# A gated recurrence feeding four expert layers: the first unit's work spread over four engines, the second group's input split earlier, and later units' scores set next to the unit ahead

## The chip, the cores and the metric

One core of one Trainium2 chip. The metric is the device time of one execution in microseconds (us), lower is better. "Start-to-start" is the time from the start of one matmul to the start of the next on TensorE, taken from the trace; a pace is its mean over a stream, without waits and half-speed stretches.

## The reference

Four batches, eight heads, 768 time steps, head width 48. A recurrence with a per-channel decay gives 3072 rows of 384; four experts with 1024 hidden columns are applied to every row and merged with normalised weights.

```python
for t in range(S):
    state = alpha[:, :, t, :, None] * state + einsum('bhd,bhe->bhde', k[:, :, t], v[:, :, t])
    y[:, :, t] = einsum('bhd,bhde->bhe', q[:, :, t], state)
x = y.transpose(0, 2, 1, 3).reshape(B * S, H * D)
p = domain_probs / (domain_probs.sum(-1, keepdims=True) + 1e-09)
for e in range(E):
    h = np.maximum(x @ w1[e], 0.0)
    out += p[:, e:e + 1] * (h @ w2[e])
```

## The kernel before

The rows are cut into 24 **units** of 128 rows (six time blocks of four batches), and the units into groups. A group's units first go through the recurrence (`attention(u)`, 17 steps that the scheduler hands out one by one), which leaves x, then through the experts. While the experts of group g run, the recurrence of group g + 1 is fed in between: `deal` gives every step of every unit a time, and `advance` emits it when the estimated clock has reached it. A step's instructions stand in each engine's program where `advance` emits them, and that place is all that a "time" means.

From the second group on, x, w1, w2 and the hidden layer are each split into three parts (w2 and the hidden layer of the second group only in part), and every product of split operands is three faster matmuls instead of a slow one (for down 3 x 175 ns, where the unsplit product shows as two records 323 ns apart). In what follows **up** is the product with w1 (512 columns of x stream, w1 is stationary) and **down** is the product with w2 (384 columns of w2 stream, the hidden layer is stationary).

The parts that the change touches:

```python
BEATS = [*(0.055 * (j + 1) for j in range(11)), 0.69, 0.75, 0.8, 0.87, 0.94, 1.0]

def attention(u):                                  # each yield ends a step
    nc.scalar.copy(out=AT, in_=turned(pair(ra)))   # turned: 4 transposes on TensorE
    ...
    nc.scalar.copy(out=KT, in_=turned(pair(rk)))
    nc.vector.tensor_mul(own, rq[:, :, :D], rk[:, :, :D])
    nc.vector.reduce_sum(out=dot, in_=own, axis=AX.X)
    yield
    nc.vector.tensor_mul(QT, turned(pair(rq)), AT)
    yield
    # seven levels: copy_q (ScalarE), next_q, next_k
    def next_q(li):
        nc.vector.tensor_mul(qv, qv, spread(dv[:, :, :, 0], m))
        dec = work.tile([P, NP, P // (2 * m)], F32, name=f"dec{li}", bufs=1)
        nc.vector.tensor_mul(dec, dv[:, :, :, 0], dv[:, :, :, 1])
    def next_k(li):
        nc.scalar.copy(out=new[:, :, :, 1, :], in_=old[:, :, :, 1, :])
        nc.vector.tensor_mul(new[:, :, :, 0, :], ...)
    ...   # scores (sc) of levels 0-3, later far (level 6) and sc of levels 4-5
    for s in range(2):                             # lat <- near
        nc.scalar.copy(out=lat[rows, :, rows], in_=near[rows])
    ...   # result (yps), keys turned back
    if cb < NCB - 1:                               # state product and update
        sps = ps.tile([P, NP, 2, D], F32, name="sps", tag="w")
        for p in range(NP):
            nc.tensor.matmul(sps[:, p], lhsT=KB[:, p, :], rhs=rv[:, 2 * p:2 * p + 2, :D], ...)
        for i in range(2):
            rows = slice(HD * i, HD * (i + 1))
            old, add = st[rows, :, i, :], sps[rows, :, i, :]
            ...
# deal(): a unit's window [begin, end] and its 17 steps in it
events += [(begin + (end - begin) * beat, u, run) for beat in BEATS]
# start: the constants and the domain probabilities on the ACT queue, the rest on SP
nc.scalar.dma_start(out=p_all, in_=moe_domain_probs.rearrange("(n p) e -> p n e", p=P))
load(0, "akqv"); load(1, "akqv")
# the last slot's down stage of a group: the next group's x is split in between
for step, at in enumerate((0.0, 0.6, 0.7, 0.78)):
    ... between.append((at, lambda step=step: split_x(after[0], step)))
```

The state product uses only the two diagonal blocks of what it computes: head pair p with values of both heads gives four blocks, and two are read.

## Time and profile before

| | before |
|---|---|
| time, median of 3 | 1064.21 us (1062.67 to 1064.66) |
| span of the profiled run | 1062.8 us |
| TensorE busy | 98% of it |
| first expert matmul | 26.22 us |
| up matmuls of 512 columns, start-to-start | 229.8 ns, 1440 of them |
| down matmuls with split operands, start-to-start | 175.0 ns, 1872 of them |

The prediction shows the table by stretches: its columns are the stretch, its length, then busy us and instructions of TensorE, of weight loads, VectorE, ScalarE and GpSimd, then granted clock, DMA share and GB/s.

```profile
150.00:175.00 25.00, 22.89 (x139) 15.36 (x138) 20.55 (x41) 13.81 (x32) 2.68 (x5) 0.93 1.01 380
```

The number to look at is 0.93: in these 25 us TensorE's granted clock was not full.

The timeline of an up stream (start, duration, engine, line, work):

```profile
517.92 1.53 PE L546 MATMUL one<-xT,w 128*128 128x512 f32 x6
...
519.98 1.53 PE L546 MATMUL one<-xT,w 128*128 128x512 f32 x6
```

Nine matmuls take 519.98 - 517.92 = 2.06 us. A stream's pace is read from starts like these. The busy time of the group hides it: it counts overlapping durations.

### The profile page before, as it was taken

The numbers are of one execution on the slowest core, as the hardware profiler recorded it, in microseconds if no ns is written. First come the engines' busy times: TensorE is split into PE (matmuls) and PEld (weight loads), VectorE is DVE, ScalarE is ACT, GpSimd is POOL, SyncE is SP. The second block draws the span as 40 slices with busy tenths as digits, with TensorE's granted clock in tenths as the row PEclk, the third lists the DMA queues.
The fourth block names the chain that finished last, engine by engine and source line by source line (L and its number), as shares of the span: only waits on it lengthen the run. The fifth ranks groups of instructions, "written<-read, shape, count | busy, mean of one in ns | idle before, by whom it ended". The sixth has DMA issues, their size and how long they took to land.

```text
span 1062.8 us, 21599 instructions
## 1 busy us (share of the span) xinstructions
PE 1041.9 (98%) x8508; PEld 906.2 (85%) x8508; DVE 781.6 (74%) x1619; ACT 569.0 (54%) x1202; POOL 32.9 (3%) x71
## 2 busy tenths in 40 slices
PE   8899999999999999999999999999999999999998
PEld 7777776687788898898898998988989889898988
DVE  5488777677779877778877877986877875666565
ACT  5687875665756555536546435555464443323232
POOL 2010010000001000000000000000000000000000
PEclk9999999999999999999999999999999999999999
DMA  8596799797977957758669559586594454444531
GB/s 124 157 325 202 245 318 352 272 339 241 307 256 271 376 180 276 279 165 315 249 187 364 201 190 339 172 307 231 167 373 174 194 208 170 187 179 178 197 160 45
DMA packets 158838, 251.66 MB, mean 237 GB/s; under 512 B 120113, under 2 KB 135345, under 8 KB 136209
## 3 DMA queue, kind: packets, MB, share of 16 engines
q1 hardware_dynamic: 149600, 208.82, 57.3%
q0 software_dynamic: 5760, 41.29, 9.7%
q8 instruction: 67, 1.10, 0.4%
q10 hardware_dynamic: 3376, 0.17, 0.3%
q14 instruction: 35, 0.28, 0.1%
HBM read 207.79 MB, written 42.47 MB: 235 GB/s over the span
## 4 chain that ended last, share of the span: by engine, by line
PE 85%; ACT 5%; DVE 5%; DMA 2%; issue 2%; SPq 1%; ACTq 0%; DVEq 0%
PE ops L639 36%; PE one L546 23%; PE two L546 11%; PE sc L338 6%; PE yps L432 3%; PE tp L270 3%; ACT qb L312 2%; PE one L538 1%; PE sps L467 1%; PE far L393 1%; DMA hT<-in_moe_w_dram 1%; DVE w L230 1%; ACT KT L330 1%; DMA rq<-in_q_dram 1%; SPq L214 1%
## 5 line engine op out<-in xcount | busy, mean ns | idle before, releaser
L639 PE MATMUL ops<-w,hT 128*128 128x384 f32 x1872 | 347.4, 340 | 0.2 <-DVE hT L592 0.2
L639 PEld LDWEIGHTS ops<-w,hT 128*128 128x128 f32 x1872 | 325.4, 188 | 4.7 <-ACT t L557 0.6
L546 PE MATMUL one<-xT,w 128*128 128x512 f32 x960 | 254.4, 400 | 2.7 <-DVE xT L252 2.3
L546 PEld LDWEIGHTS one<-xT,w 128*128 128x128 f32 x960 | 176.3, 189 | 42.2 <-DVE xT L252 4.0
L557 ACT ACTIVATE t<-one 128x512 f32<-128x512 f32 (+1 forms) x192 | 107.2, 558 | 180.7 <-PE one L546 175.3
L312 ACT COPY qb<-QT 64x256 f32<-64x256 f32 x336 | 136.6, 407 | 71.2 <-DVE QT L293 42.7
L586 DVE SCALAR_TENSOR_TENSOR hT<-t,hT 128x512 fp32r<-128x512 f32 (+1 forms) x172 | 110.5, 643 | 68.3 <-ACT hT L584 65.8
L559 DVE TENSOR_TENSOR t<-t,two 128x512 f32<-128x512 f32 (+1 forms) x172 | 109.5, 636 | 58.0 <-ACT t L557 29.3
L584 ACT ACTIVATE hT<-t 128x512 fp32r<-128x512 f32 (+1 forms) x172 | 101.8, 592 | 86.4 <-DVE t L559 85.3
L546 PE MATMUL two<-xT,w 128*128 128x512 f32 x480 | 136.9, 394 | 0.0
L546 PEld LDWEIGHTS two<-xT,w 128*128 128x128 f32 x480 | 90.6, 189 | 20.2 <-DVE acc L668 0.2
L639 PE MATMUL ops<-hT 128*128 128x384 f32 x288 | 100.9, 491 | 0.3 <-DMA hT<-in_moe_w_dram 0.3
L592 DVE SCALAR_TENSOR_TENSOR hT<-hT 128x512 fp32r<-128x512 f32 (+1 forms) x172 | 101.0, 634 | 0.0
L348 DVE COPY_PREDICATED near<-masks,sc 128x256 f32<-128x256 uint8 x144 | 76.9, 534 | 19.2 <-PE sc L338 16.3
L319 DVE TENSOR_TENSOR QT<-QT,dec 128x256 f32<-128x256 f32 x144 | 60.8, 423 | 36.0 <-ACT qb L312 35.3
L338 PEld LDWEIGHTS sc<-qb,KT 128*64 128x64 f32 x2304 | 72.7, 138 | 9.3 <-issue 4.7
L338 PE MATMUL sc<-qb,KT 128*64 128x64 f32 x2304 | 77.2, 223 | 2.6 <-ACT qb L312 2.6
L639 PEld LDWEIGHTS ops<-hT 128*128 128x128 f32 x288 | 52.1, 190 | 29.6 <-DMA hT<-in_moe_w_dram 0.9
L668 DVE SCALAR_TENSOR_TENSOR acc<-ops,p_all,acc 128x384 f32<-128x384 f32 x82 | 49.9, 615 | 30.4 <-PE ops L639 29.2
L330 ACT COPY KT<-KT 128x256 f32<-128x256 f32 x144 | 60.0, 417 | 3.1
L331 DVE TENSOR_TENSOR KT<-KT,dec 128x256 f32<-128x256 f32 x144 | 60.2, 418 | 0.0
L538 PE MATMUL one<-xT,w 128*128 128x256 f32 (+1 forms) x240 | 46.2, 340 | 0.6 <-ACT xT L448 0.6
(88 smaller groups left out, 934.2 us busy)
## 6 DMA issues: line engine op xcount, KB each, us to landing
w<-kept SPq DMA_DIRECT2D x144, 1152.0 KB
kept<-w POOLq DMA_DIRECT2D x32, 1152.0 KB, 7.9
hT<-in_moe_w_dram SPq DMA_DIRECT2D x32, 384.0 KB
w<-in_moe_w_dram SPq DMA_DIRECT2D x48, 128.0 KB
ra<-in_alpha_dram SPq DMA_DIRECT2D x23, 192.0 KB
rk<-in_k_dram SPq DMA_DIRECT2D x23, 192.0 KB
rq<-in_q_dram SPq DMA_DIRECT2D x23, 192.0 KB
out_dram<-acc POOLq DMA_DIRECT2D x18, 192.0 KB, 7.9
```

Source lines behind the costliest of these rows:

```text
L312: nc.scalar.copy(out=qb[rows, :, i, :].rearrange("p a (b r) -> p a b r", r=m), in_=qv[rows])
L319: nc.vector.tensor_mul(qv, qv, spread(dv[:, :, :, 0], m))
L330: nc.scalar.copy(out=new[:, :, :, 1, :], in_=old[:, :, :, 1, :])
L338: nc.tensor.matmul(out[HALF * s:HALF * (s + 1), 2 * p:2 * p + 2, :], lhsT=KTs[li][:, p, HALF * s:HALF * (s + 1)], rhs=qbs[li][:, p, :, QUA ...
L348: nc.vector.copy_predicated(near.rearrange("p a (b two r) -> p a b two r", two=2, r=m)[:, :, :, 1, :], mk.unsqueeze(1).broadcast_to([P, H, ...
L546: nc.tensor.matmul(out, lhsT=w[:, part, kc], rhs=x_part(gi, part, kc), start=(part == terms[0] and kc == 0), stop=(part == terms[-1] and k ...
L557: nc.scalar.activation(out=t, in_=one, func=ACT.Copy, scale=FINE)
L559: nc.vector.tensor_add(t, t, two)
L584: nc.scalar.activation(out=top, in_=x, func=ACT.Relu, scale=TRIM)
L586: nc.vector.scalar_tensor_tensor(out=low, in0=x, scalar=0.0, in1=top.bitcast(F32), op0=ALU.max, op1=ALU.subtract)
L592: nc.vector.scalar_tensor_tensor(out=dif, in0=top.bitcast(F32), scalar=1 / 4096.0, in1=low.bitcast(F32), op0=ALU.mult, op1=ALU.subtract)
L639: nc.tensor.matmul(sums[at], lhsT=h, rhs=w, start=(n == begins[at]), stop=(n == ends[at]))
```

## The change

It has four parts. **Start:** the first unit's work is spread over four engines (key copies to GpSimd, one copy to VectorE, two VectorE operations behind QT), and the load of the probabilities moves behind the units' loads on the SP queue. **Second group's x:** the splits start at 0.3 instead of 0.6 of the last down stage. **Later units:** new step times put a unit's scores beside the result and the state update of the unit ahead, and the state product is cut into half-width tiles that compute only the blocks that are read. **Offset:** four more buffers of a small tile shift x in SBUF.

```diff
+    IN_PAIRS = [*(0.0425 * (j + 1) for j in range(8)), 0.385, 0.43, 0.475, 0.52, 0.6, 0.67, 0.755, 0.84, 1.02]
+    TOGETHER = ((15, 7), (16, 11))
+    pairs_from = half + 2 * B + 1
...
+        alone = u == 0
+        if not alone:
+            own_terms()
         yield
         nc.vector.tensor_mul(QT, turned(pair(rq)), AT)
+        if alone:
+            own_terms()
...
-            dec = work.tile([P, NP, P // (2 * m)], F32, name=f"dec{li}", bufs=1)
+            dec = work.tile([P, NP, P // (2 * m)], F32, name=f"dec{li}", bufs=1 + 4 * (li == 6))
...
-                nc.scalar.copy(out=new[:, :, :, 1, :], in_=old[:, :, :, 1, :])
+                copy = nc.gpsimd.tensor_copy if alone else nc.scalar.copy
+                copy(out=new[:, :, :, 1, :], in_=old[:, :, :, 1, :])
...
-            nc.scalar.copy(out=lat[rows, :, rows], in_=near[rows])
+            copy = nc.vector.tensor_copy if alone and s else nc.scalar.copy
+            copy(out=lat[rows, :, rows], in_=near[rows])
...
+            apart_ = u + 1 >= pairs_from
+            sps = ps.tile([P, NP, 1 if apart_ else 2, D], F32, name="sps", tag="w")
             for p in range(NP):
-                nc.tensor.matmul(sps[:, p], lhsT=KB[:, p, :], rhs=rv[:, 2 * p:2 * p + 2, :D],
-                                 start=True, stop=True)
+                for i in range(2) if apart_ else [slice(0, 2)]:
+                    rows = slice(HD * i, HD * (i + 1)) if apart_ else slice(0, P)
+                    nc.tensor.matmul(
+                        sps[rows, p], lhsT=KB[:, p, rows],
+                        rhs=rv[:, 2 * p + i, :D] if apart_ else rv[:, 2 * p:2 * p + 2, :D],
+                        start=True, stop=True)
...
-            first = wanted[gi - 1] if gi > 1 else 0.0
+            first = wanted[gi - 1] - MARGIN * (2 < gi < LAST - 1) if gi > 1 else 0.0
...   # deal(): a unit's steps 7 and 11 are set to the times of steps 15 and 16 of the unit ahead
...
-        nc.scalar.dma_start(out=p_all, in_=moe_domain_probs.rearrange("(n p) e -> p n e", p=P))
...
         load(1, "akqv")
+        nc.sync.dma_start(out=p_all, in_=moe_domain_probs.rearrange("(n p) e -> p n e", p=P))
...   # five fewer rounds of filling matmuls at the start
-                    for step, at in enumerate((0.0, 0.6, 0.7, 0.78)):
+                    for step, at in enumerate((0.0, 0.3, 0.42, 0.54) if gi == 0 else
+                                              (0.0, 0.6, 0.7, 0.78)):
```

More of the change, by code (lines that the diff above doesn't have):

```diff
@@ L286, in attention, with own_terms @@
         nc.scalar.copy(out=KT, in_=turned(pair(rk)))
-        own = work.tile([P, NT], F32, name="t")[:, :H * D].rearrange("p (h d) -> p h d", d=D)
         dot = work.tile([P, H], F32, name="dot")
-        nc.vector.tensor_mul(own, rq[:, :, :D], rk[:, :, :D])
-        nc.vector.reduce_sum(out=dot, in_=own, axis=AX.X)
-        load(after, "k")
+        def own_terms():
+            own = work.tile([P, NT], F32, name="t")[:, :H * D].rearrange("p (h d) -> p h d", d=D)
+            nc.vector.tensor_mul(own, rq[:, :, :D], rk[:, :, :D])
+            nc.vector.reduce_sum(out=dot, in_=own, axis=AX.X)
+            load(after, "k")
+        alone = u == 0
+        if not alone:
+            own_terms()
         yield
         nc.vector.tensor_mul(QT, turned(pair(rq)), AT)
+        if alone:
+            own_terms()
         load(after, "q")
@@ L464, in attention @@
             KB = AT
-            sps = ps.tile([P, NP, 2, D], F32, name="sps", tag="w")
+            apart_ = u + 1 >= pairs_from
+            sps = ps.tile([P, NP, 1 if apart_ else 2, D], F32, name="sps", tag="w")
             for p in range(NP):
-                nc.tensor.matmul(sps[:, p], lhsT=KB[:, p, :], rhs=rv[:, 2 * p:2 * p + 2, :D],
-                                 start=True, stop=True)
+                for i in range(2) if apart_ else [slice(0, 2)]:
[4 more added lines that the diff above has]
+                        start=True, stop=True)
             for i in range(2):
                 rows = slice(HD * i, HD * (i + 1))
-                old, add = st[rows, :, i, :], sps[rows, :, i, :]
+                old, add = st[rows, :, i, :], sps[rows, :, 0 if apart_ else i, :]
                 if cb == 0:
@@ L692, in deal @@
         events = []
+        times = []
         t = 0.0
@@ L713, in deal @@
                 run = attention(u)
-                events += [(begin + (end - begin) * beat, u, run) for beat in BEATS]
+                pairs = u >= pairs_from
+                beats = [0.0, *(IN_PAIRS if pairs else BEATS)]
+                due_at = {-1: begin, **{j: begin + (end - begin) * beats[j + 1] for j in (7, 11, 16)}}
+                for ahead, j in TOGETHER if pairs else ():
+                    if (u > pairs_from or j == 11) and abs(times[-1][ahead] - due_at[j]) < space / 6:
+                        due_at[j] = times[-1][ahead]
+                marks = sorted(due_at)
+                times.append([])
+                for lo, hi in zip(marks, marks[1:]):
+                    times[-1] += [due_at[hi] if j == hi else
+                                  due_at[lo] + (due_at[hi] - due_at[lo]) * (beats[j + 1] - beats[lo + 1])
+                                  / (beats[hi + 1] - beats[lo + 1]) for j in range(lo + 1, hi + 1)]
+                for j, ahead in ((6, 13), (12, 15)):
+                    if times[:-1]:
+                        times[-1][j] = max(times[-1][j], times[-2][ahead] + 0.5)
+                events += [(time, u, run) for time in times[-1]]
         return sorted(events, key=lambda x: x[:2])
@@ L751 @@
         runs = [attention(u) for u in range(len(groups[0]))]
-        fill(8)
-        for u, n in ((0, 3), (0, 6), (0, 4), (0, 5), (0, 5), (0, 4), (0, 3), (1, 0), (0, 0), (0, 2),
+        fill(7)
+        for u, n in ((0, 2), (0, 3), (0, 4), (0, 5), (0, 5), (0, 4), (0, 3), (1, 0), (0, 0), (0, 2),
                      (0, 2), (1, 2), (0, 2), (1, 0), (0, 0), (0, 4), (0, 4), (0, 0)):
```

## The prediction

> **What bounds the kernel now.** I read the page first (busy shares, chain of waits), then the table by stretches, then the timeline of the two places that the diff names, and last the groups by line.
>
> From the page of the kernel before (engine, busy us, share, instructions; then the chain by engine):
> ```profile
> PE 1041.9 (98%) x8508; PEld 906.2 (85%) x8508; DVE 781.6 (74%) x1619; ACT 569.0 (54%) x1202; POOL 32.9 (3%) x71
> ...
> PE 85%; ACT 5%; DVE 5%; DMA 2%; issue 2%; SPq 1%; ACTq 0%; DVEq 0%
> ```
> TensorE is the bound: 98% busy, and 85% of the chain that ended last. So only two kinds of change can pay: TensorE must do less, or its few holes must close. The table by stretches says where those holes are:
> ```profile
> 180.00:1062.80 882.80, 877.91 (x6860) 775.18 (x6859) 654.83 (x1330) 443.25 (x921) 17.16 (x32) 1.00 0.65 236
> ```
> After 180 us TensorE idles 882.80 - 877.91 = 4.9 us in all. The other 16 us of its idle time (1062.8 - 1041.9 = 20.9) lie before 180 us. Busy hides waits inside a stream of matmuls, too, so I also looked at start-to-start times.
>
> The first hole is the start (start us, us, engine, line, work, [idle before <- releaser], from the timeline):
> ```profile
> 8.61 0.56 DVE L289 TENSOR_TENSOR t<-rq,rk 128x384 f32<-128x384 f32 x1 [8.61 <-DMA rq<-in_q_dram]
> ...
> 9.21 0.55 DVE L290 TENSOR_REDUCE dot<-t 128x8 f32<-128x384 f32 x1
> ...
> 9.68 0.68 DVE L293 TENSOR_TENSOR QT<-tp,AT 128x512 f32<-128x512 f32 x1
> ...
> 11.34 0.45 ACT L330 COPY KT<-KT 128x256 f32<-128x256 f32 x1
> 11.35 0.43 DVE L319 TENSOR_TENSOR QT<-QT,AT 128x256 f32<-128x256 f32 x1 [0.99 <-ACT qb L312]
> ...
> 23.24 1.24 ACT L410 COPY lat<-near 64x512 f32<-64x512 f32 x2 [1.14 <-DVE near L348]
> ```
> Nothing useful happens on VectorE until q lands at 8.61; the first two operations then stand ahead of QT, which everything hangs on. The first real matmul of the expert layers starts at 26.22.
>
> The second hole is the change to the second group (timeline):
> ```profile
> 165.66 0.50 PE L546 MATMUL one<-xT,w 128*128 128x512 f32 x1 [0.17 <-DVE xT L252]
> ...
> 166.99 0.50 PE L546 MATMUL one<-xT,w 128*128 128x512 f32 x1 [0.83 <-DVE xT L252]
> ...
> 168.32 2.08 PE L546 MATMUL one<-xT,w 128*128 128x512 f32 x4 [0.83 <-DVE xT L252]
> ```
> TensorE gets one part of x, waits, gets the next. From start to start 1.33 us passes where 0.23 is normal.
>
> The third thing is the two groups that the later units' change concerns:
> ```profile
> 145.29 1.03 PE L467 MATMUL sps<-rv,AT 128*128 128x96 f32 x8
> ...
> 156.32 2.08 PE L338 MATMUL sc<-qb,KT 128*64 128x64 f32 x64
> ```
> The state product (8 records; each f32 matmul shows as two) holds TensorE for 0.81 us net: I took the time from the matmul ahead of it to the one behind it after 180 us (1039 ns, the same in 11 cases to 6 ns) less one normal 229. The 64 score records hold it for 2336 - 229 = 2107 ns alone.
>
> **What the Trainium skill says.** (1) "DMA: Bandwidth & Descriptors", section "Queues, rings and completion order": each DMA engine serves its queue rows in turn, packet by packet. The trace agrees: from 4 to 7 us the ACT queue's 16-byte packets of the domain probabilities (3,072 of its 3,376 packets) run among the SP queue's packets of k and q. SP packets drop from 962 and 894 per us (at 2 and 3 us) to 248, 470 and 577 in the next three. (2) "TensorEngine Tiling (Array Packing)", section "Key Properties": changing the tiling mode drains TensorE. The trace agrees: full to narrow adds about 90 ns to the start-to-start time (322 for 229), narrow back to full shows 152 to 203. (3) "TensorE: Matmul & The Clock Gate", section "LDWEIGHTS": a weight load costs by its columns, not its rows. The trace agrees: the state product's 96-column matmuls still start 109 to 112 ns apart, like the 128-column transposes. (4) "SBUF — State Buffer", section "SBUF: two separate sides": GpSimd and VectorE share a port pair exclusively, and a VectorE operation with two SBUF inputs loses it to a GpSimd one that reads SBUF. No run here shows it yet; GpSimd only does memsets and DMA issues in this trace.
>
> **The change part by part.**
>
> *Start.* The probabilities' load moves from the ACT queue to SP, behind both units' loads. The 3,072 packets of a, k and q then run at some 930 a us from 2.0 us on and are through at 5.3 instead of 6.95; q landed 1.65 us after its last packet, so it lands near 7.0: **-1.6 us**. The two operations ahead of QT (0.56 + 0.55) move behind it; QT must still wait for its transposes (8.65 + 0.63), so that gives 9.68 - 9.35 = 0.33, of which some 0.15 returns because they now delay the next VectorE step. One of the two 0.62 us copies of L410 goes to VectorE and runs beside the other: about -0.4. The KT copies to GpSimd give nothing: at 11.34 ACT's 0.45 us copy runs beside VectorE's 0.43 us product, which the next qb copy waits for anyway. Sum -2.2 us for the first expert matmul (26.2 to about 24). But the last quarter of w1 is issued until 23.17 and its packets run to some 28.5 us; with 1.5 us of latency it lands near 30. TensorE wanted it at 30.8 before and would want it at 28.6: a stall of over a us there, part of which replaces the 1.29 us wait for AT at 31.5. I count **-1.8 us**. The five fewer rounds of filling matmuls only take up the shorter wait.
>
> *Second group's x.* The waits at 165 to 169 us are (661 - 323) + (1328 - 229) + (1330 - 229) + (594 - 229) = 2.9 us. The splits move from 0.6 to 0.3 of the last down stage, before the slot's end. But their 6 VectorE operations (4.1 us) now stand ahead of the last split of a w1 piece (160.46), whose store and reload the matmuls need at about 178; part of the gain can turn into that wait. I count **-1.8 us**.
>
> *Later units.* Working the two schedules' arithmetic through gives the order of TensorE's groups (it reproduces the 15 result-to-scores neighbours in the trace before). Result and first scores were already neighbours for 15 of the units and become so for 17; at 4003 ns together against 1988 + 2336 - 229 apart, a pair saves only 0.09 us. What is new is that the state product of units 10 to 19 runs in half-width column tiles, in the mode of the scores, and (but for unit 17) directly ahead of the next unit's far scores. It becomes 16 records like the scores', (2107 - 220 for entry and exit) / 64 = 29.5 ns each, 0.47 us instead of 0.81. 9 x 0.34 + 0.12 for unit 17, which pays entry and exit by itself: **-3.2 us**. The number of visits to a narrow mode stays 56, because before the state product ran in full mode between full-mode matmuls and switched nothing.
>
> *Offset.* The decay tile's five buffers cost SBUF, and the count looks chosen so that x stays where it was against w1: in the program before x lies at 96 and w1 at 32 modulo 128, 64 apart, and the title says 64 after. The up matmuls should stay at 2.06 us per nine (229 ns): **0**.
>
> Sum: -1.8 - 1.8 - 3.2 - 0.1 = -6.9 us, 1064.2 to 1057.3.
>
> **The rivals.** *GpSimd costs more than it saves.* VectorE is busy 1.1 to 1.3 us of each 1.41 us level at the start, mostly with two-input operations; if each GpSimd copy locks it out, six levels could lose 0.2 to 0.3 us each, 1.5 us, and the start would gain next to nothing: 1059. Against it: the copies have slack before the scores need them. *The start's gain is not held up.* If w1 also lands earlier or the stall falls in other waits, the start gives 3 us or more, and later waits for ACT and VectorE (1 to 2 us each before 90 us) shrink with it: 1054. *The gathered steps overload ACT and VectorE.* Units now do more in less time, with TensorE in order behind them; VectorE is at 0.7 to 0.9 in most stretches. If each of 13 units makes TensorE wait 0.5 us, the later gain is gone: 1063. For it: some later waits of 0.5 to 0.9 us exist (349 and 825 us). Against it: 4.9 us of idle in 880. *The offset matters.* If x did move against w1, 1440 up matmuls at 3 ns each would be 4.3 us, in either direction.
>
> **Range and chances.** The parts are small and fairly independent: start -0.5 to -3.5, x 0 to -2.9, state product -2 to -3.5, collisions 0 to +4. That gives **1057.3 us**, with 1052 to 1062 to hold 8 times in 10. 2% is 21 us, more than all holes of TensorE; **faster by over 2%: 0.01, within 2%: 0.98, slower by over 2%: 0.01**.
>
> **What would show it.** q landing near 7.0 and the first expert matmul near 24; a wait for w1 near 28 to 30; no starts 1.33 us apart at 165, but perhaps a wait on w at fc 6 of that stage; state-product records in 128*64 form, 160 becoming 240 with 160 of them narrow at some 30 ns; the up stream still 2.06 us per nine. It would be wrong if the up stream changes pace, if TensorE shows more than 3 us of new waits after 250 us, or if the early gain is swallowed by a DMA wait at 142 to 154 us, where the chain hangs on w2 for 12 us.

## The result, and the profile after

The changed kernel took 1058.97 us (median of 4, 1058.81 to 1060.18) against 1063.84 (4 runs, 1062.67 to 1064.66). The ratio is 0.9958, 95% interval 0.9940 to 0.9975: 0.4% less, which is "the same" at the 2% mark. A ratio here is the mean time of one kernel's fast runs over that of the other's of the same rounds, so it is not quite the ratio of the medians. The profiled run of the changed kernel was the slowest of its four (1060.18 us, span 1058.4), so the two traces differ by 4.4 us.

From the page after (busy time; chain of waits; one DMA queue):

```profile
PE 1038.4 (98%) x8578; PEld 900.9 (85%) x8578; DVE 779.6 (74%) x1620; ACT 566.6 (54%) x1195; POOL 35.5 (3%) x77
...
q10 hardware_dynamic: 288, 0.12, 0.1%
...
PE 88%; DVE 3%; DMA 3%; ACT 3%; SPq 2%; issue 1%; POOL 0%; DVEq 0%; ACTq 0%; POOLq 0%
```

TensorE is busy 3.5 us less and is still the bound. The ACT queue (q10) had 3,376 packets before and has 288. The two stretches:

```profile
150.00:175.00 25.00, 24.63 (x187) 17.39 (x186) 21.80 (x46) 16.24 (x37) 2.69 (x5) 1.00 1.01 380
...
180.00:1058.40 878.40, 870.43 (x6916) 766.16 (x6915) 648.56 (x1320) 439.13 (x910) 17.10 (x32) 1.00 0.67 236
```

From 150 to 175 the clock is 1.00 and TensorE's holes are almost gone. After 180 its idle time rose: 878.40 - 870.43 = 8.0 us, where the kernel before has 4.9. So something was given back late.

To find where, I numbered TensorE's expert matmuls (up and down, 4,128 in order, numbered from 0, the same in both kernels) and took the times between some of them from both traces:

| stage, by the number of the expert matmul | before, us | after, us | difference |
|---|---|---|---|
| start of the span to the first | 26.22 | 24.65 | -1.57 |
| first to the 60th | 19.13 | 18.62 | -0.51 |
| 60th to the 320th | 102.56 | 102.71 | +0.15 |
| 320th to the 400th (change to the second group) | 29.34 | 25.60 | -3.74 |
| 400th to the 2,040th | 443.56 | 443.13 | -0.43 |
| 2,040th to the 3,020th | 244.07 | 246.27 | +2.20 |
| 3,020th to the last | 193.70 | 193.23 | -0.47 |
| last to the end of the span | 4.22 | 4.21 | -0.01 |

**Start.** The timeline of the changed kernel:

```profile
7.47 0.60 PE L275 MATMUL tp<-ident,rq 128*128 128x128 f32 x4
...
8.19 0.69 DVE L305 TENSOR_TENSOR QT<-tp,AT 128x512 f32<-128x512 f32 x1 [8.19 <-PE tp L275]
...
11.10 0.41 POOL L345 COPY KT<-KT 128x256 f32<-128x256 f32 x1 [3.04 <-DVE KT L346]
11.28 0.51 DVE L333 TENSOR_TENSOR QT<-QT,dec 128x256 f32<-128x256 f32 x1 [0.31 <-ACT qb L326]
...
30.42 0.49 PE L559 MATMUL one<-xT,w 128*128 128x128 f32 x2 [0.27 <-DMA w<-in_moe_w_dram]
```

QT moves from 9.68 to 8.19. At 11.28 a VectorE product runs beside a GpSimd copy and takes 0.51 us where 0.43 is normal, and one at 14.15 takes 0.62; the copy beside that one takes 0.73 us (at 13.76) where the five others take 0.40 to 0.42. So the two engines slow each other at two places, by 0.08 and 0.19 us for VectorE. That fits a shared port, but it does not show the exclusive lock that the prediction took from the Trainium skill: the product at 11.28 ended 0.27 us after the copy, less than its own 0.43 us, and one at 12.73 lost nothing although a copy ran until 12.86 (times on GpSimd are rough). The predicted wait for w1 is at 30.42.

**Change to the second group.** The same three waits of 0.17, 0.83 and 0.83 us as at 165.66 to 168.32 before are gone:

```profile
163.58 1.64 PE L567 MATMUL one<-xT,w 128*128 128x512 f32 x6
165.06 0.87 PE L567 MATMUL two<-xT,w 128*128 128x512 f32 x3
```

Nine matmuls run through from 163.58. Start-to-start times show why the gain (3.74) exceeds those waits: in the kernel before, the next six starts after 168.92 are 426 and 427 ns apart, and from 171.9 on 230. TensorE ran at half speed from the third wait on. "TensorE: Matmul & The Clock Gate" in the Trainium skill, section "What's actually happening", has 1.2 GHz, that is 427 ns for 512 columns, after at least one idle activity window of about 3.4 us. The 427 ns agree. The idle time does not reach that: three waits of 1.83 us in sum with matmuls between them. The clock that the trace records was at half from 168.19 to 171.60 us, for 3.41 us: that is the 0.93 of the table. The page calls the window free-running and the result variable from run to run; the runs below agree with both (see The experiments).

**Later units.** The groups of the state product by form (line, engine, work, count | busy us, mean ns of one | idle before), and the up stream on the timeline:

```profile
L486 PE MATMUL sps<-rv,AT 128*128 128x96 f32 x80 | 10.5, 274 | 0.3 <-ACT AT L472 0.3
...
L486 PE MATMUL sps<-rv,AT 128*64 128x48 f32 x160 | 6.7, 227 | 0.0
```

```profile
952.54 1.56 PE L567 MATMUL one<-xT,w 128*128 128x512 f32 x6
...
954.64 1.56 PE L567 MATMUL one<-xT,w 128*128 128x512 f32 x6
```

The 160 full-width records became 80 full and 160 narrow ones, as predicted; the mean duration of a narrow record is no price, since they start 30 ns apart on average, as worked out (29.5). But nine up matmuls now take 2.10 us instead of 2.06: the pace changed, which was predicted not to. And the waits of TensorE after 170 us are new ones:

```profile
PE far L408 <- DVE hT L607: 2.7, 1, 2.7
PE far L408 <- ACT qb L326: 1.2, 1, 1.2
```

The longer one on the timeline:

```profile
657.24 0.63 ACT L605 ACTIVATE hT<-t 128x512 fp32r<-128x512 f32 x1 [0.87 <-DVE t L580]
...
657.78 0.80 ACT L326 COPY qb<-QT 64x256 f32<-64x256 f32 x2
...
658.63 1.12 PE L408 MATMUL far<-qb,KT 128*64 128x128 f32 x8 [2.66 <-DVE hT L607]
...
659.54 1.92 PE L353 MATMUL sc<-qb,KT 128*64 128x64 f32 x32
```

The far scores need the last copy of q (qb). In the new step times that copy is emitted only 0.045 of a unit's window ahead of them. Here ScalarE has it behind the ReLU of the up stage's last tile, and TensorE stands for 2.66 us. Undisturbed far scores take 0.66 us and these 32 score records 1.10; here they take 1.12 and 1.92: the clock was halved again (recorded from 658.57 to 661.98, once more 3.41 us; the view by stretches has 0.81):

```profile
654.00:663.00 9.00, 6.34 (x58) 5.70 (x58) 5.83 (x14) 4.11 (x8) 0.00 (x0) 0.81 0.73 244
```

### The profile page after: what moved, and what is told of

Its sections match the earlier page's. It is cut to its first block, busy times and chain, and to the rows that moved or that the text cites. A ratio compares the mean times of both kernels' runs of the same rounds, so it can differ in the third digit from the quotient of the medians.

```text
span 1058.4 us, 21780 instructions
## 1 busy us (share of the span) xinstructions
PE 1038.4 (98%) x8578; PEld 900.9 (85%) x8578; DVE 779.6 (74%) x1620; ACT 566.6 (54%) x1195; POOL 35.5 (3%) x77
## 4 chain that ended last, share of the span: by engine, by line
PE 88%; DVE 3%; DMA 3%; ACT 3%; SPq 2%; issue 1%; POOL 0%; DVEq 0%; ACTq 0%; POOLq 0%
PE ops L660 37%; PE one L567 23%; PE two L567 11%; PE sc L353 6%; PE tp L275 3%; PE yps L448 3%; PE one L559 2%; DMA w<-in_moe_w_dram 1%; DMA hT<-in_moe_w_dram 1%; ACT qb L326 1%; PE far L408 1%; PE sps L486 1%; SPq L219 1%; PE idle L788 1%; DMA rq<-in_q_dram 1%
## 5 line engine op out<-in xcount | busy, mean ns | idle before, releaser
L345 ACT COPY KT<-KT 128x256 f32<-128x256 f32 x138 | 57.5, 417 | 5.0 <-PE sc L353 1.9
```

## The experiments

The first four kernels ran on one chip beside 11 runs of the kernel before (median 1063.2, 1061.01 to 1064.44), the next four on another (11 runs, 1063.32, 1061.96 to 1065.29). The changed kernel itself did not run in these rounds. "Above the change" below is the distance of a median to its 1058.97; from the intervals of the two ratios I estimate that such a distance is known to about 2 us.

One more thing has to be compared like with like. Each of the seven traces with a mean granted clock of 0.998 has exactly one spell of 3.41 us at half clock in mid-kernel, and the seven at 0.999 and 1.000 have none. Three of the changed kernel's four runs were at 1.000 (1058.81 to 1059.00 us), so where a variant ran mostly at 0.998 or less, part of its distance is spells. I give the runs at 1.000 beside the median.

The clock changes that the traces record also tell when a spell comes. In all seven, it begins a whole number of 3.41 us steps (47 to 192) after the run's first moment at full clock, so the steps form a fixed grid. In the step just before each spell TensorE had idled for 1.67 to 2.60 us (by its records, whose ends are modelled). Of the other steps after the first 14 us of the 14 traces, none had more than 1.57 us of idle time, but for one of 2.02 us in a_both that no spell followed. So about half a step of idle time brings a spell, with that one exception, and the same wait can fall into one step or be shared by two.

**Theory:** the pace of a matmul stream depends on where the moving operand lies against the stationary one. From the program's addresses: before, x lies 64 bytes beyond w1 and w2 192 beyond the hidden layer modulo 256; after, 192 and 64. Five buffers of 16 bytes came out as 32 each, so x moved by 128 bytes. Modulo 128, which I used in the prediction, nothing changed. **Rivals:** x's own address counts; or the slower up stream comes from the new step order. And for the new waits, theory: the late q copy; rival: gathering overloads the engines anyway.

### b_shift: the offset alone

```diff
-            dec = work.tile(..., name=f"dec{li}", bufs=1)
+            dec = work.tile(..., name=f"dec{li}", bufs=1 + 4 * (li == 6))
```
(on the kernel before)

> The kernel before with nothing but the decay tile's five buffers, so x, the x staging tile and the hidden tiles lie 128 bytes further on (x minus w1 goes from 64 to 192 modulo 256, w2 minus hidden from 192 to 64). Theory A, the pace of a stream of matmuls follows the distance of the moving from the stationary operand modulo 256, 64 fast and 192 slow: up starts 229.8 to 233.3 ns apart (1440 x 3.5 = +5.0 us), down 175.0 to 173.4 (1872 x -1.66 = -3.1 us), together +1.9 us, 1065.7. Theory B, the slower up stream of the changed kernel comes from its busier schedule: up stays at 229.8 and down at 175.0, 1063.8.

Measured: 1065.71 us (1063.55 to 1066.5), ratio 1.0023 [1.0008, 1.0038]. Up 233.2 ns, down 173.4. The offset alone makes the kernel slower, by changing both paces, without any new step order. (1440 x 3.5 ns = +5.0 us for up; 1872 x -1.65 = -3.1 us for down; +1.9 us together.)

### b_gap: x moved as much, and w1 with it

```diff
         for i in range(NQ):
             load_piece(0, i)
+        wts.tile([P, 32], F32, name="gap", bufs=1)
```
(on the kernel before: 128 bytes between w2 and w1)

> The kernel before with 128 unused bytes between the w2 and w1 tiles: x and w1 both move by 128 (x minus w1 stays 64), the hidden tiles move and w2 does not (w2 minus hidden goes from 192 to 64). Theory A (distance modulo 256): up stays at 229.8 ns, down falls to 173.4: -3.1 us, 1060.7. Theory C (the address of x by itself modulo 256 counts): x lies where it is slow, up goes to 233.3: 1065.7 or so. Theory B: no change.

Measured: 1062.14 us (1060.12 to 1063.93), ratio 0.9994 [0.9980, 1.0009]. Up 230.7 ns with x at the very address of b_shift, down 173.35. So for up the address of x alone does not set the pace: with w1 moved along, up keeps (nearly) its pace at distance 64. Down gains, as w2 is now 64 beyond the hidden layer; but w2 lies at the same address modulo 256 in all kernels here, so for down the runs cannot tell the distance from the hidden layer's own address. The expected gain in time does not stand out of the scatter: the point is -0.6 us, and the interval includes none. That the time follows the pace I therefore take from b_shift, from the last run, and from the runs of the next one at full clock.

### a_both: the change with both distances at 64

```diff
-... bufs=1 + 4 * (li == 6))
+... bufs=1 + 8 * (li == 6))
+        wts.tile([P, 32], F32, name="gap", bufs=1)
```
(on the kernel after; the second line stands where b_gap has it)

> The changed kernel with nine decay buffers and the 128 unused bytes between w2 and w1: x minus w1 is 64 and w2 minus hidden 64. Theory A: up 229.8 ns, down stays 173.4: -5.0 us against the changed kernel, 1054.0. Theory B: 1059, up stays at 233.3.

Measured: 1057.21 us (1054.48 to 1060.92), ratio 0.9948 [0.9929, 0.9967]; up 230.8, down 173.3, as expected. The total missed. Its two runs with a mean granted clock of 1.000 took 1054.48 and 1054.98; the four at 0.997 to 0.998 took 1057.17 to 1060.92. The two are 4.2 us under the change's runs at 1.000, where the pace alone (1440 x 2.4 ns) gives 3.5. One of the four is the profiled one, and its waits and timeline show what happens in it:

```profile
PE one L567 <- DMA w<-kept: 2.0, 1, 2.0
```

```profile
165.07 2.18 PE L567 MATMUL one<-xT,w 128*128 128x512 f32 x6 [2.01 <-DMA w<-kept]
167.05 1.48 PE L567 MATMUL two<-xT,w 128*128 128x512 f32 x3
```

With x ready early, TensorE comes early to a piece of w1 that is still on its way back from device memory. It waits 2.01 us, and 0.84 us later the clock halves: nine matmuls take 3.3 us for 2.1. The changed kernel's own profiled run has no such wait at that place, so it comes and goes from run to run. (a_both's run has the far wait of 2.7 us too, and its clock stayed up there.)

### a_lead: the last q copy a little earlier

```diff
-    IN_PAIRS = [..., 0.385, 0.43, 0.475, 0.52, 0.6, ...]
+    IN_PAIRS = [..., 0.365, 0.395, 0.425, 0.52, 0.6, ...]
```
(on the kernel after)

> The changed kernel with steps 8 to 10 of a unit earlier (0.365, 0.395, 0.425 for 0.385, 0.43, 0.475), so the last q copy is emitted about twice as far ahead of the far scores that read it. Theory: the 2.7 and 1.2 us waits of the far scores at 656 and 831 us come from that short lead behind ScalarE's queue at the end of an up stage; they go, -3.5 us, 1055.5. Rival: the waits come from the total load on ScalarE and VectorE there; they move elsewhere or stay, within 1 us of 1059.

Measured: 1056.38 us (1055.96 to 1058.02), ratio 0.9943 [0.9929, 0.9957]. Both far waits are gone; what waits are left after 170 us sum to 0.8 us. The stage from the 2,040th to the 3,020th matmul falls from 246.27 to 241.50 us. The same place on its timeline:

```profile
654.04 0.81 ACT L326 COPY qb<-QT 64x256 f32<-64x256 f32 x2
...
656.43 0.63 ACT L605 ACTIVATE hT<-t 128x512 fp32r<-128x512 f32 x1 [1.58 <-DVE t L580]
...
657.22 0.66 PE L408 MATMUL far<-qb,KT 128*64 128x128 f32 x8
...
657.70 1.10 PE L353 MATMUL sc<-qb,KT 128*64 128x64 f32 x32
```

The q copy now stands ahead of the ReLU, and far and scores run at full speed. The overload rival falls: the same gathering, with the copy earlier, has no such wait. In the trace the place cost 2.66 us of waiting and 1.25 of slow clock (far to the start of the matmul behind the scores: 658.63 to 661.39 after, 657.22 to 658.73 here). The medians differ by 2.6 us, less than the stage's 4.8. The change's profiled run was the one of its four at clock 0.998, and 1.2 us slower than the rest; and a_lead's trace gives back 1.0 us between the 400th and the 2,040th matmul (444.09 us for 443.13).

### a_wide: the state product at full width again

```diff
-            apart_ = u + 1 >= pairs_from
+            apart_ = False
```
(on the kernel after)

> The changed kernel with the state product of all units at full width again (4 matmuls of 96 columns for 8 of 48), everything else as it is. Theory: the narrow form is what the later units gained, 9 x 0.34 + 0.12 = 3.2 us, so 1059.0 becomes 1062.2; the two waits of the far scores (656 and 831 us) stay. Rival: the narrow form gains nothing, since visits to a narrow mode cost as much as it saves: within 1 us of 1059.

Measured: 1062.73 us (1061.74 to 1063.68), ratio 0.9996 [0.9984, 1.0008]; 3.8 us above the change. Its timeline, then the change's, at the same visit:

```profile
357.53 0.86 PE L567 MATMUL two<-xT,w 128*128 128x512 f32 x3
358.23 1.03 PE L486 MATMUL sps<-rv,AT 128*128 128x96 f32 x8
...
360.71 1.67 PE L567 MATMUL one<-xT,w 128*128 128x512 f32 x6
```

```profile
357.94 0.86 PE L567 MATMUL two<-xT,w 128*128 128x512 f32 x3
358.74 0.67 PE L486 MATMUL sps<-rv,AT 128*64 128x48 f32 x16
...
360.72 1.67 PE L567 MATMUL one<-xT,w 128*128 128x512 f32 x6
```

The far and the 32 score records stand between these lines in both. From the first line's start to the last line's, the wide form takes 3.18 us and the narrow one 2.78: 0.40 us per visit. The nine visits of this kind are the same to a few ns (2307 against 2707 ns without the matmuls ahead), and the lone product of unit 17 takes 922 ns instead of 1039. 9 x 0.40 + 0.12 = 3.7 us by the trace. The three runs at full clock have a median of 1061.85, 2.9 us above the change's, so 3.7 and 3.8 agree better than these runs can tell.

Note what is compared: a wide product directly ahead of narrow scores, which the kernel before does not have either. There the product and the scores stood apart, for (1040 - 230) + (1787 - 175) = 2422 ns of TensorE; in the changed kernel they hold it for 2306 - 233 = 2073 ns together. Against the kernel before, the step gained 0.35 us per visit, 9 x 0.35 + 0.12 = 3.3 us.

### a_x06: the second group's x at the old times

```diff
-... enumerate((0.0, 0.3, 0.42, 0.54) if gi == 0 else
+... enumerate((0.0, 0.6, 0.7, 0.78) if gi == 0 else
```
(on the kernel after)

> The changed kernel with the second group's splits back at 0.6, 0.7 and 0.78. Theory: the 1.33 us steps at the start of the second group's up stage come back, +2.9 us, with a run in which the clock falls there some 1.4 us more: 1061.5 to 1063. Rival: with the earlier splits the same time is lost waiting for w, so that the undoing costs less than 1 us: 1059 to 1060.

Measured: 1062.75 us (1060.53 to 1063.95), ratio 0.9997 [0.9984, 1.0010]; 3.8 us above the change. The steps are back:

```profile
163.53 0.50 PE L567 MATMUL one<-xT,w 128*128 128x512 f32 x1 [0.17 <-DVE xT L257]
164.86 0.50 PE L567 MATMUL one<-xT,w 128*128 128x512 f32 x1 [0.83 <-DVE xT L257]
166.19 1.20 PE L567 MATMUL one<-xT,w 128*128 128x512 f32 x4 [0.83 <-DVE xT L257]
```

Here the four matmuls after the third wait take 1.20 us, not 2.08: this run's clock stayed up, and the stage takes 27.84 us, 2.2 more than after. The waits alone are worth that; a half-speed spell comes on top in runs that have it. Its one run with a mean clock of 1.000 took 1060.53 us, 1.6 above the change's at that clock, and the four at 0.996 to 0.998 took 1062.06 to 1063.95. That is no support for a spell at the second group in those four: in the profiled one (0.998) the only spell lies at the far wait, 660.11 to 663.52 us. Sure from this run is that the waits come back and cost 1.6 to 2.2 us.

### a_start: the start undone

```diff
-        alone = u == 0
+        alone = False
+        nc.scalar.dma_start(out=p_all, ...)      # back on the ACT queue
-        nc.sync.dma_start(out=p_all, ...)
-        fill(7)      # and the old numbers of filling matmuls
+        fill(8)
```
(on the kernel after)

> The changed kernel with the start as before: the probabilities on the ACT queue ahead, the two VectorE operations ahead of QT, KT copies and both lat copies on ScalarE, 8, 3 and 6 fills. Theory: the start gave 2.1 us by the 60th expert matmul and all of it lasts: 1061.1, the first QT product at 9.7 for 8.2 us. Rival: the waits for w at 30, 152 and 164 us take it back by 200 us: 1059.5.

Measured: 1061.97 us (1060.88 to 1063.81), ratio 0.9991 [0.9979, 1.0003]; 3.0 us above the change. QT is at 10.24, the first expert matmul at 26.77. The far waits of 2.7 and 1.2 us stay, so they do not come from the start. That the start's gain lasts to the end is shown, its size is not: the one run at full clock (1060.88) is 1.9 us above the change's, and of the 2.1 us at the first expert matmul the two traces, both at 0.998, keep 1.4 at the end. The run undoes all steps of the start at once, so it does not say what each of them gave.

### a_beats: the old step times, with the narrow state product

```diff
-                pairs = u >= pairs_from
+                pairs = False
```
(on the kernel after)

> The changed kernel with the old beats for all units and nothing put together, the state product still narrow and still at the units' new pace. Theory: the gathering itself gives next to nothing (a lone narrow state product pays some 0.22 us of entry and exit, 9 x 0.22 = 2.0 us) and costs the two waits of the far scores (3.5 us): 1057.5. Rival: standing together is where the gain lies: 1061 or more.

Measured: 1060.56 us (1060.49 to 1064.93), ratio 0.9985 [0.9972, 0.9998]; 1.6 us above the change although its far waits are gone. That lies between what the two theories expected. Gathering must then be worth more than the far waits took back, but the profiled run was this kernel's slowest by 3.6 us (with a wait for w1 of 2.4 us at the second group), so the trace cannot split the sum. Five of its six runs were at full clock, so spells do not explain the 1.6. One part can be read: a lone narrow product and lone scores hold TensorE for (928 - 233) + (1787 - 175) = 2307 ns, the gathered ones for 2073, so nine visits lose 2.1 us, as the theory had it. With 3.9 us of far waits gone it should still have been 1.8 us faster than the change. Where those 3.4 us lie is not found. **Inconclusive** on the size; it does show that gathering is no loss.

### d128_0, d0_128, d96_32: other distances

All three are the change with a_lead's step times, the gap of b_gap and `apart_ = True` for every unit; they differ only in the number of buffers that shift x:

```diff
+... bufs=1 + 10 * (li == 6))    # d128_0: up 128, down 0
+... bufs=1 + 6 * (li == 6))     # d0_128: up 0, down 128
+... bufs=1 + 9 * (li == 6))     # d96_32: up 96, down 32
```

> The kernel with the 128-byte gap, the longer lead, the narrow state product for all units, and x minus w1 at 128, w2 minus hidden at 0 modulo 256. Only the pace of the streams is asked. If the pace falls smoothly from 192 to 64, 128 lies between (up 231 to 232 ns) and 0 as well (down 174.2). If only 64 is good, both are slow: up 233, down 175. If 0 means the same lines and is worst, down is over 176.

> As d128_0, but x minus w1 at 0 and w2 minus hidden at 128. The same distances change places: whichever of 0 and 128 slows the up stream should slow the down stream in the other run, if it is the distance that counts and not the tile.

> As d128_0, but x minus w1 at 96 and w2 minus hidden at 32: whether 64 is the best or one end of a range. Near 64 I expect up 229.5 to 231.5, down 173 to 174; a wide plateau would show 230.5 and 173.3.

Measured, one run each, state unknown: 1054.74, 1052.74 and 1059.14 us (the kernel before on that chip: 1063.49). With all other traces, the start-to-start times by distance modulo 256 bytes (moving operand minus stationary operand) are:

| distance | up (512 columns), ns | down (384 columns), ns |
|---|---|---|
| 0 | 228.1 (d0_128), 228.0 (d0_64) | 173.7 (d128_0) |
| 32 | | 175.1 (d96_32) |
| 64 | 229.8 (before), 230.7 (b_gap), 230.8 (a_both) | 173.3 to 173.4 (after, b_shift, b_gap, a_both, d0_64) |
| 96 | 233.3 (d96_32) | |
| 128 | 232.5 (d128_0) | 175.7 (d0_128) |
| 192 | 233.2 (after, b_shift, a_lead) | 175.0 (before) |

One outcome that I had allowed for was distance 0 as the worst; it is the best for up. 0 and 64 are good for both streams; 96, 128 and 192 are bad for up, and 32, 128 and 192 for down. There is no smooth slope. That 256 is the modulus fits the runs: at distances that are 64 and 320 modulo 512 the up stream has the same pace (b_gap 230.7, a_both 230.8), at 64 and 192 it has not.

### d0_64: the best of what was found

```diff
-    IN_PAIRS = [..., 0.385, 0.43, 0.475, ...]
+    IN_PAIRS = [..., 0.365, 0.395, 0.425, ...]
-... bufs=1 + 4 * (li == 6))
+... bufs=1 + 6 * (li == 6))
-            apart_ = u + 1 >= pairs_from
+            apart_ = True
+        wts.tile([P, 48], F32, name="gap", bufs=1)
```
(on the kernel after; the gap is now 192 bytes)

> The three findings in one kernel: x minus w1 at 0 and w2 minus hidden at 64 modulo 256, the longer lead to the far scores, the narrow state product for all units. If the pace follows each stream's own distance: up 228.1 ns, down 173.4 ns, and against the run with 0 and 128 another 1872 x -2.35 = -4.4 us: span near 1047, time near 1049, some 14 us (1.3%) under the kernel before. Rival: the good paces do not add up in one program, up above 230 or down above 174.5, 1053 or more.

Measured: **1048.92 us** (4 runs, 1048.37 to 1050.41) beside 1063.56 for the kernel before (7 runs, 1062.24 to 1065.51), ratio 0.9864 [0.9848, 0.9880]. It beats both kernels, by 14.6 and 10.1 us. Up 228.0 ns, down 173.3. The timeline of its up stream:

```profile
950.10 1.52 PE L567 MATMUL one<-xT,w 128*128 128x512 f32 x6
...
952.14 1.52 PE L567 MATMUL one<-xT,w 128*128 128x512 f32 x6
```

Nine up matmuls take 2.04 us; TensorE is still busy 98% of a span of 1046.8 us. Against the change: 1440 x 5.25 ns = 7.6 us from the pace, and 2.6 us that a_lead measured, give 10.2 for the measured 10.1. That is closer than it should be: `apart_ = True` for the earlier units was not measured apart, and by the traces their products lose 0.12 to 0.23 us each (a lone one takes 920 ns here, 1044 in the change), some 1.5 us more.

## Why the prediction was right, and where not

The time (1057.3 predicted, 1058.97 measured) lay in the range, and the class was right. One term was mis-sized, one step failed, and one allowance was used up. Of the three signs of being wrong that the prediction names, two came true: the up stream changed pace, and TensorE shows 3.9 us of new waits after 250 us. So the number held better than the account behind it.

- **TensorE is the bound, and 2% is out of reach of its holes:** held. It stayed at 98%.
- **Start, -1.8:** the sum held, two parts of it less well. In the traces -1.57 at the first expert matmul, where -2.2 was worked out, and -2.1 by the 60th; undoing it costs 1.9 (full clock) to 3.0 (medians). The first expert matmul comes at 24.02 to 24.99 us in the ten traces that have the new start, so the 24 that was predicted is within that scatter. The mechanism showed: the ACT queue's packets gone, QT 1.5 us earlier, short waits for w1 at 30 us. q's transposes started at 7.47, later than the 7.0 worked out. The stall for w1, forecast as over a us, cost 0.7 us by start-to-start times (353 and 541 ns where 112 is normal), while the wait for AT fell from 1.29 to 0.25 us: so the start gained after the first matmul where a loss was expected. The first rival, that GpSimd costs what it saves, falls: the VectorE products beside its copies lose 0.08 and 0.19 us, and the start still gained.
- **Second group's x, -1.8:** the term was mis-sized. The stage lost 3.74 us. Of the waits (2.9 us by start-to-start times in the prediction) no part had turned into a wait for w1 in this profiled run, and the sum left out that TensorE ran at half speed after them: six matmuls of 427 ns where 230 is normal are 1.2 us. With the 2.9 us that makes 4.1, for 3.74 measured. A repeat is not sure to gain so much: it depends on the spell, and b_gap, where the same three waits fell on two steps, has none. The granted clock of 0.93 could have told me before. The allowance for a wait on w1 was not wrong in kind: a_both, a_lead and a_beats have it, 1.4 to 2.4 us long, in their profiled runs.
- **State product, -3.2:** held. 0.35 us per visit for 0.34, 3.3 in all against the kernel before; a_wide, which leaves the wide product beside the scores, is 2.9 to 3.8 slower.
- **Result beside scores, -0.1:** the order of TensorE's groups came out as the step arithmetic gave it (17 neighbours; two more pairs at 0.09 would be 0.2); such an effect is below what these runs resolve.
- **Offset, 0:** this step failed, as the prediction put it: "The up matmuls should stay at 2.06 us per nine (229 ns)". They went to 2.10. I had compared addresses modulo 128 because the change's title does. The runs show that where the operands lie modulo 256 sets the pace: up +5.0 us, down -3.1, net +1.9. The fourth rival had the size (3 ns each) right for up and did not think of down.
- **Collisions, 0 to +4:** used to the end. The two far waits cost 3.9 us, and in the profiled run 1.25 more at half clock. The third rival named ScalarE and VectorE work that gathers, but put it as a load spread over 13 units. It was one step time, and moving it by 0.05 of a window removed both waits.
- **Reading (3) from the Trainium skill:** the trace shows equal paces for 96 and 128 streamed columns. It has no weight load of fewer rows, so "not its rows" is not shown here.

So the sum was near partly by luck: the second group's x brought 1.9 us more than predicted, the offset took 1.9 and the collisions stood 3.9 above the zero of the centre. From the 400th matmul on the parts add up to -3.3 + 1.9 + 3.9 + 1.25 - 0.9 (the waits of before of 0.5 and 0.4 us at 349 and 825 us, which went) = +2.9, and the traces show +1.3; some 1.6 us of this stays unassigned.

**What stays open.** What in the hardware lies behind the distance; I measured the pace at six distances and no mechanism. Whether down follows the distance or the hidden layer's own address. Why b_gap and a_both, at distance 64 for up, run 1 ns slower than the kernel before at 64: x lies at 96 modulo 256 in them and at 224 before, so the distance is perhaps not all. What decides whether a run has the wait for w1, and why one half-idle step in a_both was followed by no spell. And the split of a_beats.

## What to carry to other kernels

When a kernel is one long stream of matmuls, read its pace from start to start, per kind of matmul, and note where the two operands lie against each other modulo 256 bytes: by the pace, moving them by at most 192 bytes was worth 7.6 us here, more than any single reordering. When work is gathered to sit beside other work, look at what each gathered step needs last and on which engine that stands in line; a copy emitted a little too late cost more than the gathering's merge could save. And look at the granted clock wherever TensorE waits: a wait of 2 us can cost another 1.2 us soon after it.

## What the Trainium skill lacked or had wrong

- "TensorE: Matmul & The Clock Gate", section "Step-by-step: what each phase is for", says that loading the next tile's weights "doesn't steal SBUF read bandwidth from the running matmul". The runs show a pace that depends on the distance of the two operands modulo 256 bytes: 228.0 to 233.3 ns for 512 columns and 173.3 to 175.7 for 384, at full granted clock. No page has this. That the weight load is what takes the time is not shown.
- The same page, section "What's actually happening": half speed follows an idle window of about 3.4 us. Here it followed a single wait of 2.66 us and one of 2.01, and three of 0.17, 0.83 and 0.83 us in 3 us (none of these in every run). What the seven spells have in common is a step of 3.41 us in which TensorE idled for 1.67 us or more; one step of 2.02 us had no spell after it.
- "SBUF — State Buffer", section "SBUF: two separate sides": that GpSimd and a VectorE product with two SBUF inputs get in each other's way agrees, but "the other fully blocks" does not fit all of it: beside copies of 0.4 us, VectorE products of 0.43 us took 0.51 and 0.62 us, and one lost nothing.
- "TensorEngine Tiling (Array Packing)", section "Key Properties", gives no size for the change of mode. In this trace it is about 90 ns on entry (322 for 229 ns), so that a narrow product of 16 short matmuls saves 0.35 us against the wide one when it joins a visit that is made anyway and 0.12 when it makes its own.
